# Eleven result sums from accumulating transfers to VectorE, and shorter engine costs in a list scheduler, in a fused attention and MLP kernel

## The chip, the cores and the metric

The kernel runs on one core of a Trainium2 chip. The metric is the device time of one execution in microseconds. Three executions of the kernel before took 1354.43, 1355.80 and 1355.89 us; the median is 1355.8 us.

## The reference

Inputs are q, k, v (8 batches, 8 heads, 576 tokens, 64 wide), phi (32 memory slots) and four weight matrices. All is float32.

```
a = softmax(phi over the 32 slots); k_m = a^T k; v_m = a^T v        # per batch and head
x = softmax(q k_m^T / 8) v_m                                        # 4608 tokens x 512
h = x @ w_in;  g = s * relu(h)^2 + b;  x = g @ w_out                # 512 -> 2048 -> 512
h = x @ moe2_w_in;  g = h * sigmoid(1.702 h);  out = g @ moe2_w_out # 512 -> 2048 -> 512
```

## The kernel before, in words

The work has four stages. Stage 1 does the attention and the first product (batch by batch), stage 2 the second matrix, stage 3 the third, stage 4 the fourth, which gives `out`. In stages 2 to 4 the tokens go in N = 6 blocks `s` of 768 (two halves of TS = 384), and the matrix product of a block is made from products of half-size blocks, with sums and differences of the operands ahead and of the results behind, so that fewer products are needed. Each product is made of three matmuls per tile (high part by high, high by low, low by high), since the operands are split into a rounded part `oh` and a rest `ol` (`operand`, with `hi` on ScalarE or VectorE and `lo` on VectorE, L275, L276 and L281).

In stage 4 the method `last` (one call per block) places the products 1, 6, 7, 5, 3 and 4 of the block. The middle blocks (1 to 4) take the order 1, 6, 7, 5, Y, A, 4, B, D of the table MID, where Y, A, B and D are the steps of a product that a pair of neighbouring blocks shares (`phase4`). Products 1, 6, 5 and 3 add up in the PSUM tile X, products 7 and 4 in the PSUM tile Y, the shared steps in the PSUM tile Z. A pass of the table is 58.5 / 7 = 8.36 us long in the plan.

What leaves PSUM is written in `leaves` (one call per product) and at the end of `phase4`. In the kernel before:

- after product 1, 6, 5 or 3, ScalarE copies X to the tiles a, u2, u4 or c12 (L1235), and SyncE's queue sends them to `out` (L265);
- after product 7 ScalarE copies Y to the tile y7 (L1242; two halves at L1245 in the last block), which is sent to the quarter (1, 1) of `out`. After product 5 the tile u4 is added onto that same quarter by an accumulating transfer (`onto`, L270), issued from POOL's queue;
- after product 6 the tile u2 is sent to the quarter (1, 0), and after product 4, in all blocks but the last, ScalarE copies Y to the tile y4 and a second accumulating transfer adds it there. In the last block VectorE adds Y to u2 in two halves, and these are sent;
- the shared product Z is copied to tiles z by ScalarE (L1344, L1347) and added to `out` by 29 accumulating transfers of 192 KB. The change leaves these as they are.

So there are 11 accumulating transfers of whole quarters (384 KB each): 6 of u4 and 5 of y4.

The order of all instructions on all engines and queues is made by the class `Order` when the program is built: a list scheduler. Every operation has a due time, one or more ways (an engine with a cost in us), what it reads and writes, and the SBUF or PSUM tiles that it needs. `Order.sort` walks through time, asks for each ready operation when its engine, its operands and its tiles will be free, and takes the earliest; the due times break ties. `FIRST` (100) lowers the rank of operations that empty PSUM, so that they come ahead of others. Tiles of SBUF come from two pools: 30 of weights ("w") and 33 of all else ("t"). A tile counts as free when the end of its last use is past. The end of an operation is its start, its cost and an extra: 3.0 us for SyncE's transfers ("sync") and 5.0 us for accumulating transfers ("acc"), 0 for the others. For "acc" the cost is KB / 200: 0.96 us for 192 KB. Costs of ScalarE and VectorE come from `act` and `dve`. A wrong estimate does no harm to the result, since every real wait is on semaphores; but each engine's queue keeps the order that the plan gave it.

Of the kernel before, what the change touches and what calls it, by code (L numbers as in the profile page):

```python
# [15 lines left out]
ALU = mybir.AluOpType  # L16
AX = mybir.AxisListType
PSUM = bass.MemoryType.PSUM
P = 128
# [8 lines left out]
class Order:  # L28
# [7 lines left out]
    FILL, AHEAD, SLACK = 2.5, 190.0, 0.3  # L36

    NEAR = 10

    LAG = {"pe": 0.7, "sync": 2.5, "acc": 2.5, "dve": 0.25, "act": 0.25, "pool": 0.25}  # L40
    WEIGHT = {"dve": 2.0, "pool": 1.6, "act": 1.0}

    def __init__(self, bufs):
# [24 lines left out]
    def sort(self):  # L68
# [13 lines left out]
        at, end, on, out = {}, [0.0] * len(ops), [None] * len(ops), []  # L82
# [8 lines left out]
        while ready:  # L91
            can = {}
            limit = ready[0][0] + self.AHEAD
            for due, n in ready:
                if due > limit and can:
                    break
                _, ways, deps, new = ops[n]
                t0 = 0.0
                if new:
                    ok = True  # L100
                    for tag in {x[0] for x in new}:
                        mine = [x for x in new if x[0] == tag]
                        f = free[tag]
                        if len(f) < len(mine) or any(x not in queue[tag][:len(f)] for x in mine):
                            ok = False
                            break
                        t0 = max(t0, f[0] if len(mine) == 1 else heapq.nsmallest(len(mine), f)[-1])
                    if not ok:
                        continue
                best = None  # L110
                for i, (eng, cost, _, port) in enumerate(ways):
                    t = max(t0, at.get(eng, 0.0))
                    if port:
                        t = max(t, held["dve" if eng == "pool" else "pool"])
                    for d in deps:
                        e = end[d] + (self.LAG[eng] if on[d] != eng else 0.05)
                        if e > t:
                            t = e
                    score = t + cost * self.WEIGHT.get(eng, 1.0)
                    if best is None or score < best[0]:  # L120
                        best = score, t, eng, i
                can.setdefault(best[2], []).append((best[1], due, n, best[3]))
            if not can:
                raise RuntimeError("no order")
            first = []
            for tag, v in can.items():
                t0 = min(v)[0]
                like = [c for c in v if c[0] <= t0 + 0.1 and c[2] in self.narrow and c[1] >= self.since] if tag == "pe" and run else ()
                if like:
                    c = min(like, key=lambda c: c[1:])  # L130
                    if c[1] < min(v, key=lambda c: c[1:])[1] + self.NEAR:
                        first.append(c)
                        continue
                first.append(min((c for c in v if c[0] <= t0 + (self.SLACK if c[1] < self.until else 0.0)), key=lambda c: c[1:]))
            t, _, n, i = min(first)
            _, ways, _, new = ops[n]
            eng, cost, fn, port = ways[i]
            if port:
                held[eng] = t + cost
            if self.fill and eng == "pe":  # L140
                out.append(lambda n=int((t - at.get(eng, 0.0)) * self.FILL): self.fill and self.fill(n))
            for x in new:
                queue[x[0]].remove(x)
                heapq.heappop(free[x[0]])
            at[eng], on[n] = t + cost, eng
            end[n] = t + cost + (3.0 if eng == "sync" else 5.0 if eng == "acc" else 0.0)
            ready.remove((rank[n], n))
            if eng == "pe":
                run = n in self.narrow
            out.append(fn)  # L150
            for m in after[n]:
                left[m] -= 1
                if not left[m]:
                    bisect.insort(ready, (rank[m], m))
            for x in of[n]:
                last[x] = max(last[x], end[n])
                uses[x] -= 1
                if not uses[x]:
                    heapq.heappush(free[x[0]], last[x] + 0.2)
# [5 lines left out]
class Net:  # L165
# [33 lines left out]
    TS, N = 384, 6  # L199
# [48 lines left out]


    def act(self, n, fn, psum=False, count=1):  # L250
        return "act", count * ((166 if psum else 195) + 0.835 * n) / 1e3, fn, False

    def dve(self, n, fn, fast=False, count=1, port=False):
        return "dve", count * (120 + 0.6 * n if fast else (150 + 1.045 * n) if port else (60 + 1.04 * n)) / 1e3, fn, port

    def pe(self, due, n, fn, r=(), w=(), count=0, narrow=False):

# [52 lines left out]
    def convert(self, due, key, out, src, lead=6, pool=True):  # L310
# [10 lines left out]
        def size(act):  # L321
            H = T[raw][:, :, 1]
            m = to["m"] = out().bitcast(U32)
            if act:
                nc.scalar.activation(m.bitcast(F32), H.bitcast(F32), AF.Abs)
            else:
                nc.vector.tensor_scalar(m, H, 0x7FFFFFFF, None, op0=ALU.bitwise_and)

        def low(act):
            L = T[raw][:, :, 0]  # L330
            if act:
                nc.scalar.activation(L, L, AF.Copy, scale=2.0 ** -29)
            else:
                nc.vector.tensor_scalar(L, L, 2.0 ** -29, None, op0=ALU.mult)
# [827 lines left out]
    HEAD = {1: -2, 6: 0, 7: 1, 5: 2, "Y2": 3, 3: 4.5, 4: 5.5}  # L1162
    MID = {1: -3, 6: 0, 7: 1.25, 5: 2.25, "Y": 3.25, "A": 4.75, 4: 5.25, "B": 6.25, "D": 7.75}
    END = {1: -3, 6: 0, 7: 1.25, 5: 2.25, "A2": 3.25, 3: 3.75, "B2": 4.75, 4: 5.25, "D2": 5.75}
    AHEAD, OD, CC, RAW = 10, 6, 5, 4
    LONG = {"Y": 0.5, "A": 0.5, "B": 0.5, "D": 0.25}
    EARLY, LEAD, BEGIN, T4 = 8, 8, -2, -6.3

# [58 lines left out]
    def leaves(self, s, i, X, Ys, d):  # L1227

        nc, T, TS = self.nc, self.T, self.TS
        n = 2 * TS  # L1230
        a, u2, u4, c12 = (("t", (x, "w2", s)) for x in ("a", "u2", "u4", "c12"))
        alone = s in (0, self.N - 1)

        def copy(k):
            self.on_act(d, n, lambda: nc.scalar.copy(self.two(k), T[X][:, :, 0:TS]), (X,), ((*k, 0), (*k, 1)), self.FIRST, psum=True)  # L1235

        def send(k, i, j):
            self.dma(d + 1, lambda: self.a["out"][s, i, j], lambda: T[k].rearrange("p a b -> p (a b)"), ((*k, 0), (*k, 1)), (("out", s, i, j),), 384)

        def seven(k):  # L1240
            if Ys[0] == Ys[1]:
                self.on_act(d, n, lambda: nc.scalar.copy(self.two(k), T[Ys[0]][:, :, 0:TS]), (Ys[0],), ((*k, 0), (*k, 1)), self.FIRST, psum=True)  # L1242
                return
            for o in range(2):
                self.on_act(d, TS, lambda o=o: nc.scalar.copy(self.get(k, [P, 2, TS])[:, o], T[Ys[o]][:, o, 0:TS]), (Ys[o], *(((*k, 0),) if o else ())), ((*k, o),), self.FIRST, psum=True)  # L1245

        def plus(k, i, j):
            self.onto(d + 1, lambda: self.a["out"][s, i, j], lambda: T[k].rearrange("p a b -> p (a b)"), ((*k, 0), (*k, 1)), (("out", s, i, j),))

        y7, y4 = (("t", ("y", "w2", s, i)) for i in (7, 4))  # L1250
        if i == 1:
            copy(a)
            if s < self.N - 1:
                send(a, 0, 0)
            else:
                self.dma(d + 1, lambda: self.a["out"][s, 0, 0][:, TS:2 * TS], lambda: T[a][:, 1], ((*a, 1),), (("out", s, 0, 0),), 192)
        elif i == 6:
            copy(u2)
            if Ys[0] == Ys[1]:
                send(u2, 1, 0)  # L1260
        elif i == 7:
            seven(y7)
            send(y7, 1, 1)
        elif i == 5:
            copy(u4)
            if not alone:
                send(u4, 0, 1)
            plus(u4, 1, 1)
        elif i == 3:
            copy(c12)  # L1270
            send(c12, 0, 1)
        elif i == 4 and Ys[0] == Ys[1]:
            seven(y4)
            plus(y4, 1, 0)
        elif i == 4:
            for o in range(2):
                self.tt(d, TS, lambda o=o: T[u2][:, o], lambda o=o: T[Ys[o]][:, o, 0:TS], lambda o=o: T[u2][:, o], ALU.add, (Ys[o],), ((*u2, o),), self.FIRST)
                self.dma(d + 1, lambda o=o: self.a["out"][s, 1, 0][:, o * TS:o * TS + TS], lambda o=o: T[u2][:, o], ((*u2, o),), (("out", s, 1, 0, o),), 192)

    def phase4(self, s, m, w, due, st, G):  # L1280
# [258 lines left out]
```

## Time and profile before

| | before |
|---|---|
| median of three runs | 1355.8 us |
| time of the profiled execution | 1355.95 us |
| its span (first to last instruction) | 1354.2 us |
| PE (matmuls) busy | 1333.3 us, 98% |
| VectorE (DVE) busy | 1112.5 us, 82% |
| ScalarE (ACT) busy | 865.2 us, 64% |
| GpSimd (POOL) busy | 87.3 us, 6% |
| mean transfer rate | 284 GB/s |

Busy times are sums over instructions that overlap with those of other engines, so they don't add up to the span. The busy time of PE counts a matmul from its start to its modelled end; a busy PE is one that had a matmul in work. The transfer that an instruction of POOL's queue issues is carried out later by the DMA engines: from issue to landing. In the trace, the stages begin at about 0, 297, 644 and 997 us.

### The profile page before, as it was taken

The numbers are of one execution on the slowest core, as the hardware profiler recorded it, in microseconds if no ns is written. First come the engines' busy times: TensorE is split into PE (matmuls) and PEld (weight loads), VectorE is DVE, ScalarE is ACT, GpSimd is POOL, SyncE is SP. The second block draws the span as 40 slices with busy tenths as digits, with TensorE's granted clock in tenths as the row PEclk, the third lists the DMA queues.
The fourth block names the chain that finished last, engine by engine and source line by source line (L and its number), as shares of the span: only waits on it lengthen the run. The fifth ranks groups of instructions, "written<-read, shape, count | busy, mean of one in ns | idle before, by whom it ended". The sixth has DMA issues, their size and how long they took to land. (4 is left out here: it accounts for less than half of the span.)

```text
span 1354.2 us, 24210 instructions
## 1 busy us (share of the span) xinstructions
PE 1333.3 (98%) x9078; PEld 1290.1 (95%) x9078; DVE 1112.5 (82%) x1615; ACT 865.2 (64%) x1213; POOL 87.3 (6%) x82
## 2 busy tenths in 40 slices
PE   7999999999999999999999999999999999999998
PEld 5888888899999999999999999999999999999998
DVE  6878996999898897989986898695477688888885
ACT  4766666788887888778654665575455455646544
POOL 2201220200000000000000000000000011101011
PEclk8999999999999999999999999999999999999999
DMA  9989999797865785498999799889999788778974
GB/s 362 354 307 345 360 342 323 267 320 267 283 192 172 227 295 164 168 354 320 382 342 353 255 345 336 321 308 334 344 332 345 227 240 248 205 221 228 285 203 92
DMA packets 151349, 384.81 MB, mean 284 GB/s; under 512 B 16832, under 2 KB 27712, under 8 KB 151232
## 3 DMA queue, kind: packets, MB, share of 16 engines
q1 hardware_dynamic: 145472, 373.24, 78.2%
q0 software_dynamic: 5760, 10.03, 5.0%
q8 instruction: 71, 1.16, 0.4%
q14 instruction: 46, 0.38, 0.1%
HBM read 232.41 MB, written 150.80 MB: 283 GB/s over the span
## 5 line engine op out<-in xcount | busy, mean ns | idle before, releaser
L305 PE MATMUL h<-ah,mh 128*128 128x288 f32 x512 | 154.6, 302 | 0.2 <-DVE ml L281 0.2
L307 PE MATMUL h<-ah,ml 128*128 128x288 f32 x512 | 151.1, 295 | 0.2 <-ACT ml L815 0.2
L306 PE MATMUL h<-al,mh 128*128 128x288 f32 x512 | 150.7, 294 | 0.0
L281 DVE TENSOR_TENSOR ol<-A,oh 128x768 fp32r<-128x768 f32 x120 | 112.5, 953 | 28.9 <-ACT oh L275 14.4
L932 PE MATMUL X<-oh,wo 128*128 128x384 f32 x384 | 128.3, 334 | 0.0
L933 PE MATMUL X<-ol,wo 128*128 128x384 f32 x384 | 128.3, 334 | 0.0
L934 PE MATMUL X<-oh,wo 128*128 128x384 f32 x384 | 128.3, 334 | 0.0
L1080 PE MATMUL X<-oh,w 128*128 128x384 f32 x384 | 128.3, 334 | 0.0
L1081 PE MATMUL X<-ol,w 128*128 128x384 f32 x384 | 128.3, 334 | 0.0
L1082 PE MATMUL X<-oh,w 128*128 128x384 f32 x384 | 128.3, 334 | 0.0
L275 ACT CAST oh<-A 128x768 fp32r<-128x768 f32 x116 | 98.1, 860 | 44.1 <-DVE A L281 8.4
L834 ACT ACTIVATE r<-h 128x576 f32<-128x576 f32 x122 | 85.8, 706 | 56.0 <-PE h L307 47.7
L1216 PE MATMUL X<-oh,w 128*128 128x384 f32 x320 | 107.0, 334 | 0.8 <-ACT u L1235 0.8
L305 PEld LDWEIGHTS h<-ah,mh 128*128 128x128 f32 x512 | 96.1, 188 | 11.5 <-issue 3.6
L1218 PE MATMUL X<-oh,w 128*128 128x384 f32 x320 | 106.9, 334 | 0.0
L1217 PE MATMUL X<-ol,w 128*128 128x384 f32 x288 | 96.4, 335 | 1.4 <-DVE ol L281 1.4
L307 PEld LDWEIGHTS h<-ah,ml 128*128 128x128 f32 x512 | 96.1, 188 | 0.4 <-ACT ml L815 0.4
L306 PEld LDWEIGHTS h<-al,mh 128*128 128x128 f32 x512 | 96.1, 188 | 0.1
L275 ACT CAST oh<-B 128x768 fp32r<-128x768 f32 x70 | 59.2, 855 | 42.3 <-DVE B L281 19.0
L275 ACT CAST oh<-C 128x768 fp32r<-128x768 f32 x67 | 58.0, 875 | 35.2 <-DVE C L281 12.5
L281 DVE TENSOR_TENSOR ol<-B,oh 128x768 fp32r<-128x768 f32 x72 | 67.7, 953 | 9.1 <-DMA out<-z 5.6
L1380 ACT ACTIVATE u<-u 128x768 f32<-128x768 f32 x48 | 40.7, 848 | 50.4 <-DVE u L281 50.4
(294 smaller groups left out, 3871.9 us busy)
## 6 DMA issues: line engine op xcount, KB each, us to landing
w<-w SPq DMA_DIRECT2D x132, 512.0 KB, 5.7
r<-r SPq DMA_DIRECT2D x128, 288.0 KB, 4.1
kv<-in_kv SPq DMA_DIRECT2D x72, 258.0 KB, 5.2
g<-u SPq DMA_DIRECT2D x48, 384.0 KB, 4.1
raw<-in_w SPq DMA_DIRECT2D x32, 512.0 KB, 5.9
q<-in_q SPq DMA_DIRECT2D x32, 288.0 KB, 5.6
A<-r SPq DMA_DIRECT2D x24, 384.0 KB, 4.6
B<-r SPq DMA_DIRECT2D x24, 384.0 KB, 4.8
```

The lines of the kernel that those rows point to most:

```text
L275: self.order.add(due, [self.act(n, lambda: nc.scalar.copy(out(), src()), psum), self.dve(n, lambda: nc.vector.tensor_copy(out(), src()), f ...
L281: self.order.add(due, [self.dve(n, lambda: nc.vector.tensor_tensor(out(), a(), b(), op=op), port=port)], r, w, first)
L305: self.nc.tensor.matmul(ps, wh, xh, start=start and i == 0, stop=False)
L306: self.nc.tensor.matmul(ps, wh, xl, start=False, stop=False)
L307: self.nc.tensor.matmul(ps, wl, xh, start=False, stop=(i == n - 1))
L932: nc.tensor.matmul(out, T[w][:, 0, c], T[h][:, p], start=f, stop=False, skip_group_check=True)
L933: nc.tensor.matmul(out, T[w][:, 0, c], T[l][:, p], start=False, stop=False, skip_group_check=True)
L934: nc.tensor.matmul(out, T[w][:, 1, c], T[h][:, p], start=False, stop=last, skip_group_check=True)
L1080: nc.tensor.matmul(out, T[w][:, 0, c], T[h][:, k], start=f, stop=False, skip_group_check=True)
L1081: nc.tensor.matmul(out, T[w][:, 0, c], T[l][:, k], start=False, stop=False, skip_group_check=True)
L1082: nc.tensor.matmul(out, T[w][:, 1, c], T[h][:, k], start=False, stop=k == 1, skip_group_check=True)
L1216: nc.tensor.matmul(out, T[w][:, 0, c], T[h][:, p], start=f, stop=False, skip_group_check=True)
```

## The change

The plan's costs for ScalarE and VectorE are shortened, and ends get a table of their own:

```diff
+    END_LAG = {"sync": 3.0, "acc": 8.0, "dve": 0.09, "act": 0.09}
...
-            end[n] = t + cost + (3.0 if eng == "sync" else 5.0 if eng == "acc" else 0.0)
+            end[n] = t + cost + self.END_LAG.get(eng, 0.0)
...
-        return "act", count * ((166 if psum else 195) + 0.835 * n) / 1e3, fn, False
+        return "act", count * ((100 if psum else 110) + 0.835 * n) / 1e3, fn, False
...
-        return "dve", count * (120 + 0.6 * n if fast else (150 + 1.045 * n) if port else (60 + 1.04 * n)) / 1e3, fn, port
+        return "dve", count * (50 + 0.6 * n if fast else (75 + 1.045 * n) if port else (60 + 1.04 * n)) / 1e3, fn, port
...
-    AHEAD, OD, CC, RAW = 10, 6, 5, 4
+    AHEAD, OD, CC, RAW = 11, 6, 5, 3
```

AHEAD and RAW are lead times in the due times of loads: a pair's older block is due 1 us earlier, the loads of the operands C and D 1 us later.

In `leaves`, the copies of Y and the accumulating transfers of u4 and y4 go; VectorE adds Y to the tile instead, and one plain transfer takes the sum out:

```diff
-        alone = s in (0, self.N - 1)
+        alone, b5 = s in (0, self.N - 1), ("t", ("b5", "w2", s))
...
-        def seven(k):
+        def plus(k, to):
             if Ys[0] == Ys[1]:
-                self.on_act(d, n, lambda: nc.scalar.copy(self.two(k), T[Ys[0]][:, :, 0:TS]), (Ys[0],), ((*k, 0), (*k, 1)), self.FIRST, psum=True)
+                if to == k:
+                    self.tt(d, n, lambda: T[k], lambda: T[Ys[0]][:, :, 0:TS], lambda: T[k], ALU.add, (Ys[0],), ((*k, 0), (*k, 1)), self.FIRST)
+                else:
+                    self.tt(d, n, lambda: self.two(to), lambda: T[Ys[0]][:, :, 0:TS], lambda: T[k], ALU.add, (Ys[0], (*k, 0), (*k, 1)), ((*to, 0), (*to, 1)), self.FIRST)
                 return
             for o in range(2):
...
+                self.tt(d, TS, lambda o=o: T[k][:, o], lambda o=o: T[Ys[o]][:, o, 0:TS], lambda o=o: T[k][:, o], ALU.add, (Ys[o],), ((*k, o),), self.FIRST)
...
-        def plus(k, i, j):
-            self.onto(d + 1, lambda: self.a["out"][s, i, j], lambda: T[k].rearrange("p a b -> p (a b)"), ((*k, 0), (*k, 1)), (("out", s, i, j),))
...
         elif i == 6:
             copy(u2)
-            if Ys[0] == Ys[1]:
-                send(u2, 1, 0)
-        elif i == 7:
-            seven(y7)
-            send(y7, 1, 1)
         elif i == 5:
             copy(u4)
-            if not alone:
+            if alone:
+                plus(u4, u4)
+                send(u4, 1, 1)
+            else:
                 send(u4, 0, 1)
-            plus(u4, 1, 1)
+                plus(u4, b5)
+                send(b5, 1, 1)
...
-        elif i == 4 and Ys[0] == Ys[1]:
-            seven(y4)
-            plus(y4, 1, 0)
         elif i == 4:
+            plus(u2, u2)
+            if Ys[0] == Ys[1]:
+                send(u2, 1, 0)
+                return
             for o in range(2):
```

So after product 7 nothing leaves PSUM; after product 5 the sum Y + u4 is made (in u4 itself in the first and last block, in a new tile b5 in the others, where u4 is sent on its own too); after product 4 the sum Y + u2 is made in u2, which is no longer sent after product 6.

## Rows read from the trace of the kernel before

**Rows 1.** Windows by stage, then one stretch of stage 4: window, length, busy time (instructions) by engine

```profile
core 0: us, PE busy (x) PEld busy (x) DVE busy (x) ACT busy (x) POOL busy (x), PEclk, DMA share, GB/s
0.00:50.00 50.00, 39.14 (x334) 32.43 (x334) 37.78 (x64) 29.66 (x49) 12.47 (x14) 0.86 0.92 344
50.00:308.00 258.00, 257.08 (x2760) 223.75 (x2759) 219.69 (x346) 176.89 (x265) 39.61 (x28) 1.00 0.94 329
308.00:997.00 689.00, 688.91 (x3994) 688.50 (x3994) 569.85 (x831) 471.51 (x644) 0.00 (x0) 1.00 0.82 289
997.00:1354.20 357.20, 348.12 (x1997) 345.43 (x1995) 285.24 (x376) 187.15 (x256) 35.26 (x40) 1.00 0.79 234
1205.00:1230.00 25.00, 23.39 (x134) 22.75 (x133) 25.00 (x39) 15.69 (x24) 2.60 (x4) 1.00 0.68 190
```

**Rows 2.** Waits of PE in stage 4: total us, times, longest

```profile
PE Z L1330 <- DVE ol L281: 1.6, 2, 0.9
PE X L1217 <- DVE ol L281: 1.4, 1, 1.4
PE Z L1329 <- ACT z L1347: 1.1, 2, 0.9
PE X L1216 <- ACT u L1235: 0.8, 1, 0.8
PE Z L1329 <- ACT u L1235: 0.3, 1, 0.3
```

**Rows 3.** Chain that ended last, pieces of stage 4: start us, us, what

```profile
1196.03 7.80 issue
...
1212.49 1.74 DVE ol L281 x2
...
1218.43 0.45 PE Z L1330
...
1236.87 4.23 issue
...
1262.12 6.48 DMA out<-y
...
1286.86 9.76 DMA out<-z
...
1350.49 0.56 DVE a L281
```

**Rows 4.** Timeline of POOL in stage 4: start, us, issue [idle before <-releaser]

```profile
1195.69 0.89 POOL L270 DMA_DIRECT2D out<-z  x1 [10.66 <-ACT z L1347]
...
1234.33 0.88 POOL L270 DMA_DIRECT2D out<-y  x1 [3.42 <-ACT y L1242]
```

**Rows 5.** Timeline of ACT, 1082 to 1100 us

```profile
1090.65 0.80 ACT L1242 COPY y<-Y 128x768 f32<-128x768 f32 x1 [7.92 <-DMA out<-u]
...
1095.52 0.80 ACT L1235 COPY u<-X 128x768 f32<-128x768 f32 x1 [1.36 <-DMA out<-y]
```

**Rows 6.** Groups of VectorE and ScalarE in stage 4, by form: busy us, mean ns | idle before

```profile
L281 DVE TENSOR_TENSOR u<-Y,u 128x768 f32<-128x768 f32 x2 | 1.9, 954 | 0.9 <-PE Y L1082 0.9
...
L275 ACT CAST oh<-A 128x768 fp32r<-128x768 f32 x66 | 54.2, 836 | 41.0 <-DVE A L281 8.4 <-issue 7.8 <-PE Y L1217 4.8
...
L1242 ACT COPY y<-Y 128x768 f32<-128x768 f32 x10 | 8.0, 798 | 10.2 <-DMA out<-u 7.9 <-PE Y L1218 2.2
L1245 ACT COPY y<-Y 128x384 f32<-128x384 f32 x2 | 1.0, 476 | 0.0
```

**Rows 7.** Transfers by issue: queue, count, KB each, median us to landing

```profile
out<-z POOLq DMA_DIRECT2D x29, 192.0 KB, 5.3
...
out<-y POOLq DMA_DIRECT2D x5, 384.0 KB, 6.7
```

**Rows 8.** Waits of VectorE in stage 4 for a load: total us, times, longest

```profile
DVE A L281 <- DMA C<-g: 9.1, 6, 3.1
```

**Rows 9.** Waits of VectorE in stage 3 (640 to 997 us)

```profile
DVE ab L281 <- PE Z L1151: 29.7, 16, 4.2
...
DVE u L281 <- PE Y L1082: 4.1, 15, 0.8
```

More of the change, by code (lines that the diff above doesn't have):

```diff
@@ L1238, in send @@
             self.dma(d + 1, lambda: self.a["out"][s, i, j], lambda: T[k].rearrange("p a b -> p (a b)"), ((*k, 0), (*k, 1)), (("out", s, i, j),), 384)
-        def seven(k):
+        def plus(k, to):
             if Ys[0] == Ys[1]:
-                self.on_act(d, n, lambda: nc.scalar.copy(self.two(k), T[Ys[0]][:, :, 0:TS]), (Ys[0],), ((*k, 0), (*k, 1)), self.FIRST, psum=True)
+                if to == k:
+                    self.tt(d, n, lambda: T[k], lambda: T[Ys[0]][:, :, 0:TS], lambda: T[k], ALU.add, (Ys[0],), ((*k, 0), (*k, 1)), self.FIRST)
+                else:
+                    self.tt(d, n, lambda: self.two(to), lambda: T[Ys[0]][:, :, 0:TS], lambda: T[k], ALU.add, (Ys[0], (*k, 0), (*k, 1)), ((*to, 0), (*to, 1)), self.FIRST)
                 return
             for o in range(2):
-                self.on_act(d, TS, lambda o=o: nc.scalar.copy(self.get(k, [P, 2, TS])[:, o], T[Ys[o]][:, o, 0:TS]), (Ys[o], *(((*k, 0),) if o else ())), ((*k, o),), self.FIRST, psum=True)
-        def plus(k, i, j):
-            self.onto(d + 1, lambda: self.a["out"][s, i, j], lambda: T[k].rearrange("p a b -> p (a b)"), ((*k, 0), (*k, 1)), (("out", s, i, j),))
-        y7, y4 = (("t", ("y", "w2", s, i)) for i in (7, 4))
+                self.tt(d, TS, lambda o=o: T[k][:, o], lambda o=o: T[Ys[o]][:, o, 0:TS], lambda o=o: T[k][:, o], ALU.add, (Ys[o],), ((*k, o),), self.FIRST)
         if i == 1:
@@ L1271, in leaves @@
             send(c12, 0, 1)
-        elif i == 4 and Ys[0] == Ys[1]:
-            seven(y4)
-            plus(y4, 1, 0)
         elif i == 4:
+            plus(u2, u2)
+            if Ys[0] == Ys[1]:
+                send(u2, 1, 0)
+                return
             for o in range(2):
-                self.tt(d, TS, lambda o=o: T[u2][:, o], lambda o=o: T[Ys[o]][:, o, 0:TS], lambda o=o: T[u2][:, o], ALU.add, (Ys[o],), ((*u2, o),), self.FIRST)
                 self.dma(d + 1, lambda o=o: self.a["out"][s, 1, 0][:, o * TS:o * TS + TS], lambda o=o: T[u2][:, o], ((*u2, o),), (("out", s, 1, 0, o),), 192)
```

## The prediction, made before the result was known

> **What bounds the kernel now.** I read the windows by stage first, since 98% busy for the whole says nothing of where the rest lies. Between 308 and 997 us PE is busy 688.91 of 689.00 us [rows 1]: 3994 matmuls, one every 0.172 us, nothing to gain. Stage 1 after its start loses 0.92 us of 258. The first 50 us lose 10.86 us while the first loads and the first batch's attention come in. Stage 4 loses 9.08 us of 357.20, and the chain ends in VectorE's last sum at 1351.05 and its transfer [rows 3], so that some 4 us of these lie behind the last matmul. PE's waits in stage 4 are the rest: 1.6 + 1.4 + 1.1 + 0.8 + 0.3 = 5.2 us in 7 waits [rows 2]. The chain also shows that the first matmul after a wait takes 0.45 us in place of 0.17 [rows 3], 0.28 us more, so the 7 waits cost 5.2 + 7 x 0.28 = 7.2 us. That is the most that stage 4 can give.
>
> Next, what stands behind each wait. The chain shows ScalarE held for 4 to 10 us at a time by transfers that still read the tile which ScalarE is to write [rows 3]; VectorE then starves and afterwards works off a backlog, and PE meets the backlog.
> - **Group A, transfers of y and u4's path**: ScalarE's copy of y waits 7.92 us for a transfer of u, and the copy of u behind it 1.36 us for one of y [rows 5]; PE loses 0.8 there [rows 2]. ScalarE's 4.23 us up to 1241.10 [rows 3] end 6.8 us after POOL issued the accumulation of y at 1234.33 [rows 4], whose median landing is 6.7 us [rows 7]; PE loses 0.2 of the 1.1 in rows 2. A plain transfer of y, 6.48 us [rows 3], is behind the 0.3. Sum 1.3 us and 3 x 0.28: 2.1 us.
> - **Group B, accumulations of z**: ScalarE's 7.80 us of "issue" up to 1203.83 [rows 3] name no releaser; they end 8.1 us after z was issued at 1195.69 [rows 4], and I put them down to it. VectorE is then busy for 25.00 of 25 us [rows 1], and PE waits twice, 1.6 us. The 9.76 us of z from 1286.86 [rows 3] stand behind 0.9 + 1.4 us. Sum 3.9 us and 4 x 0.28: 5.1 us (rounding aside, the two groups make 7.2).
>
> **The change part by part.** The profiled execution took 1355.95 us, 0.15 above the median, with a span of 1354.2; I sum against 1355.95 and take 0.15 off.
>
> *Copies and accumulations removed.* Ten copies of 798 ns and two halves of 476 ns [rows 6] leave ScalarE: 8.9 us of an engine that is idle for 357.20 - 187.15 = 170 us in stage 4 [rows 1]. That alone is worth nothing on PE's path. Eleven accumulations leave POOL's queue, 5 of y [rows 7] and 6 of u4, with 4.3 MB each of reads and writes of `out`; no tile of y or y4 exists any more that ScalarE could wait for. Group A goes: -2.1 us. Between nothing (another transfer takes the tile's place) and -2.1 I take -2.1, as three waits of three name it.
>
> *Sums added.* Ten sums of 768 columns and two halves go to VectorE, reading PSUM. The nearest row is the same sum at the end of stage 3: 954 ns [rows 6]; issued back to back VectorE takes 1.74 / 2 = 0.87 us per operation of this width [rows 3]. 11 x 0.87 = 9.6 us, of 357.20 - 285.24 = 72 us in which VectorE was idle [rows 1]. Each stands at the head of VectorE's queue until PE ends its product, and what is queued behind (the rests `ol` and the differences for the next products, for which ScalarE and PE wait) stands too. In stage 3 such sums waited 4.1 / 15 = 0.3 us for Y, and those on Z 29.7 / 16 = 1.9 us [rows 9]. So they take between 11 x 1.2 = 13 and 11 x 2.8 = 31 us of the 72. While VectorE has slack that costs PE nothing; within a catch-up like 1205 to 1230 us each 0.87 goes through. Ends: 0 and +7 (eight sums in four middle blocks, all through). I take +0.9, one sum of the eleven, since catch-ups follow from the very stalls that go.
>
> *Tiles.* u2 is now kept from product 6 to product 4, some five passes of 8.36 us of the plan, where y7 and y4 lived for some 10 us each: about half a tile of 33 more in use on average. Loads wait for tiles, and VectorE waits for loads (9.1 us in 6 waits for C [rows 8]). A half tile in 33 is 1.5%; the cover is VectorE's idle time. 0, with ends 0 and +1. The lead times AHEAD and RAW move loads by 1 us in opposite directions and count with this.
>
> *Queues.* SyncE's queue sends as many quarters as before; POOL's queue no longer holds z behind u4 and y4. Nothing on PE's path.
>
> *The reckoning.* Old costs equal durations: 195 + 0.835 x 768 = 836 ns for a cast, as in rows 6. New ones equal distances: 75 + 1.045 x 768 = 878 ns, against the 0.87 us of rows 3. So the plan drifts less from the chip. For accumulations of z it now holds the tile for 0.96 + 8 = 9.0 us from issue, not 6.0. The three holds above lasted 6.8, 8.1 and 9.8: two of them would have ended inside the 9.0, none inside the 6.0. That speaks to group B. Ends: 0 and -5.1; I take 0.6 of it, -3.1, as the 9.76 of the pair that cost most still exceeds 9.0, and which free tile is given out is not by the plan's own estimate.
>
> The Trainium skill, on the page "DMA: Bandwidth & Descriptors", section "Anatomy of one DMA — SWDGE (gpsimd) path", gives about 2.0 us and bytes / 436 GB/s for a transfer issued from GpSimd, which an estimate makes 2.5 us for 192 KB. By it the old 5 us were ample, the 8 would buy nothing, and the sum would lose its -3.1. The trace differs: a median of 5.3 us for z [rows 7] and 9.76 at the longest [rows 3].
>
> *Stages 1 to 3.* All orders are made anew, though no operation of these stages changes. Stage 2 and 3 have nothing to lose but their cover (VectorE 83% busy). The start, with 10.86 us idle, can move either way. I take 0, with ends -2 and +4 (three waits of 1.4, the longest of rows 2).
>
> *The tail.* The last block's product 4 was summed on VectorE before already: 0.
>
> Sum: -2.1 + 0.9 - 3.1 = -4.3: 1355.95 - 4.3 - 0.15 = 1351.5 us.
>
> **The rivals.**
> 1. *Only y's stalls go.* The accumulations of z hold ScalarE as before; 29 of 40 remain and the page's rule above would have it that the longer reserve is worth nothing. For it: the longest hold exceeds even 9.0 us. Against: two of three don't. -2.1: 1353.7 us.
> 2. *All stalls go.* For it: with 4.3 MB less in the slow queue z lands sooner. -7.2: 1348.6 us.
> 3. *New waits elsewhere.* A new order in 24,000 instructions opens as many waits as it closes, at the start or in stage 1. For it: the old costs, too long, left margin. Against: stages 2 and 3 have 17% of VectorE to spare. Three waits of 1.4 us on top of the forecast: 1355.7 us.
> 4. *VectorE becomes the bound (slower).* The sums stand at the head of VectorE's queue in the middle blocks, where a backlog is being worked off; from the point where the backlog is longer than the lead of the next product's operands, every 0.87 us goes to PE. 8 x 0.87 = 7.0, less 2.1: +4.9, 1360.7 us. For it: 25 us of VectorE without a gap, and the 1.9 us waits of stage 3. Against: 80% busy over the stage, and 83% is carried without loss in stage 3, which sums on VectorE in the same way.
>
> That the edit does something else can be left aside: both accumulations are gone from the code for every block.
>
> **How the numbers follow.** A measurement here can tell about 0.2%, 2.7 us: faster is below 1353.1, slower above 1358.5. Forecast (-2.7 to -6) 0.42, rival 2 0.13: faster 0.55. Rival 1 0.22, rival 3 0.11: same 0.33. Rival 4 0.12. The range goes from all stalls gone and a start better by 1 us, 1347.5, to rival 3 with 2 us more, 1357.5; it leaves out rival 4 and little else.
>
> **What would show it.** In the changed trace: no transfers out<-y, 29 accumulations left; PE's waits in stage 4 near 2 us in place of 5.2, none of them behind y; sums u<-Y and b<-Y on VectorE at 0.87 to 0.95 us. Z's landing above 9 us with ScalarE held by it speaks for rival 1. VectorE above 85% busy in stage 4, with PE waiting for `ol` behind a sum, speaks for rival 4. A first 50 us with PE busy well below 39 us, or gaps in stages 2 and 3, speak for rival 3. PE's waits in stage 4 no shorter than before would make the prediction wrong.

## The result: 1.4% slower, and the profile after

The changed kernel takes 1373.89 us (median; 1371.77 to 1378.75), the kernel before beside it 1355.12 us (1354.37 to 1355.89): a ratio of 1.0144 with a 95% interval of 1.0113 to 1.0174. The forecast was 1351.5, its range ended at 1357.5, and its sign was wrong. The profiled execution of the changed kernel took 1375.49 us.

The page of the changed kernel, its span, the busy time of each engine, and the queue of POOL's transfers (packets, MB, share):

```profile
span 1373.7 us, 24220 instructions
PE 1342.7 (98%) x9088; PEld 1296.6 (94%) x9088; DVE 1130.5 (82%) x1634; ACT 851.4 (62%) x1194; POOL 78.1 (6%) x71
...
q0 software_dynamic: 4176, 5.70, 3.1%
```

The edit did what it says: POOL's queue moves 5.70 MB, some 4.3 MB less than before, and 29 accumulations are left, all of z. The shares do not show where 19.5 us more of span come from. The windows by stage do (columns as in [rows 1]):

```profile
0.00:50.00 50.00, 41.46 (x365) 33.80 (x366) 39.24 (x64) 31.51 (x54) 12.43 (x14) 0.90 0.95 351
50.00:308.00 258.00, 257.04 (x2745) 223.94 (x2744) 224.92 (x353) 176.25 (x264) 39.92 (x28) 1.00 0.94 328
308.00:997.00 689.00, 687.82 (x3983) 686.85 (x3982) 570.49 (x831) 465.15 (x636) 0.00 (x0) 1.00 0.82 288
997.00:1373.70 376.70, 356.34 (x2001) 352.04 (x1999) 295.87 (x389) 178.48 (x243) 25.71 (x29) 0.98 0.68 212
```

Up to 997 us the two kernels are level: PE is busy 2.3 us more in the first 50 and 1.1 us less in the stretch from 308 to 997. Stage 4 takes 376.70 us against 357.20 [rows 1]; 19.5 us, all of the loss. It has 20.4 us without PE in place of 9.1, and a mean clock of 0.98. VectorE is 295.87 / 376.70 = 79% busy, as before.

PE's waits in stage 4, changed kernel (total us, times, longest), which answer to [rows 2]:

```profile
PE X L1218 <- DVE ol L282: 5.4, 5, 2.4
PE X L1217 <- ACT u L1236: 4.9, 2, 4.0
PE X L1217 <- ACT oh L276: 2.9, 2, 2.0
PE X L1218 <- DVE D L282: 2.2, 1, 2.2
PE Z L1328 <- ACT z L1346: 0.9, 1, 0.9
PE X L1217 <- ACT z L1346: 0.3, 1, 0.3
```

16.6 us in 12 waits, against 5.2 in 7. With 0.28 us for each restart these are 20.0 us against 7.2, which explains 12.8 of the 19.5. Most of the rest is clock. The matmuls around the two waits that end at 1272 and 1278 us (start, duration, idle before):

```profile
1272.32 0.44 PE L1218 MATMUL X<-ol,w 128*128 128x384 f32 x1 [2.38 <-DVE ol L282]
...
1276.09 0.33 PE L1218 MATMUL X<-ol,w 128*128 128x384 f32 x1
1276.27 0.34 PE L1219 MATMUL X<-oh,w 128*128 128x384 f32 x1
1278.60 0.69 PE L1217 MATMUL X<-oh,w 128*128 128x384 f32 x1 [2.00 <-ACT oh L276]
1279.59 0.69 PE L1218 MATMUL X<-ol,w 128*128 128x384 f32 x1 [0.31 <-DVE ol L282]
1280.08 0.52 PE L1219 MATMUL X<-oh,w 128*128 128x384 f32 x1
1280.40 0.52 PE L1217 MATMUL X<-oh,w 128*128 128x384 f32 x1
...
1285.48 0.34 PE L1218 MATMUL X<-ol,w 128*128 128x384 f32 x1
1285.66 0.33 PE L1219 MATMUL X<-oh,w 128*128 128x384 f32 x1
```

Before 1276.27 a matmul starts every 0.17 us; after the waits, every 0.32. Read the starts, since the durations overlap. Windows of the same kernel around the three places where this happens show the clock:

```profile
1145.00:1150.00 5.00, 2.78 (x12) 2.20 (x12) 3.40 (x5) 0.59 (x2) 0.86 (x1) 0.89 0.85 246
1150.00:1155.00 5.00, 4.14 (x17) 3.69 (x15) 0.33 (x1) 1.20 (x2) 0.00 (x0) 0.77 0.63 187
...
1220.00:1225.00 5.00, 4.92 (x19) 4.92 (x20) 5.00 (x9) 1.96 (x5) 0.86 (x1) 0.66 0.50 163
...
1280.00:1285.00 5.00, 5.00 (x17) 5.00 (x17) 4.72 (x10) 0.94 (x2) 0.00 (x0) 0.50 0.10 20
```

From 1280 to 1285 the granted clock is 0.50, the lower of the two levels, 1.2 GHz: PE is "busy" for 5.00 of 5.00 us and does 17 matmuls in place of 29. Some 40 matmuls of stage 4 ran like this, each 0.15 us late: 5.9 us. In 1000 to 1345 us of before's stage 4 no 5 us were granted less than full speed. So a few long waits cost more than their length, and the busy share hides that part.

**What makes PE wait** stands two engines further back. ScalarE's waits in stage 4, changed kernel:

```profile
ACT oh L276 <- issue: 24.6, 3, 8.3
ACT oh L276 <- DVE ol L282: 24.0, 6, 8.3
```

Three times ScalarE stands for 8 us before a cast, and the trace names no releaser. Its timeline around the first, then that of VectorE and of POOL:

```profile
1139.28 0.83 ACT L276 CAST oh<-B 128x768 fp32r<-128x768 f32 x1 [8.31 <-DVE ol L282]
...
1145.12 0.47 ACT L1346 COPY z<-Z 128x384 f32<-128x384 f32 x1
1153.80 1.56 ACT L276 CAST oh<-A 128x768 fp32r<-128x768 f32 x2 [8.21 <-issue]
```

```profile
1138.29 0.96 DVE L282 TENSOR_TENSOR ol<-B,oh 128x768 fp32r<-128x768 f32 x1 [4.49 <-DMA out<-z]
...
1154.67 0.96 DVE L282 TENSOR_TENSOR ol<-A,oh 128x768 fp32r<-128x768 f32 x1 [6.26 <-ACT oh L276]
```

```profile
1145.94 0.86 POOL L271 DMA_DIRECT2D out<-z  x1 [13.59 <-ACT z L1346]
...
1204.56 0.88 POOL L271 DMA_DIRECT2D out<-z  x1 [10.87 <-ACT z L1346]
...
1269.77 0.89 POOL L271 DMA_DIRECT2D out<-z  x1 [12.84 <-ACT z L1346]
```

Read them together. ScalarE copies a half product into z at 1145.12; POOL issues its accumulation at 1145.94; by the trace's semaphore updates that lands at 1153.74; at 1153.80 ScalarE goes on. The other two landed at 1212.89 and 1277.65, and ScalarE went on at 1212.95 and 1277.71: 0.06 us after the landing each time. The addresses in the built program say why: the cast `oh` behind the copy of z was given the very tile that the accumulation of z still reads. Where VectorE's `ol` gets such a tile, VectorE itself stands, as at 1138.29. Whenever that happened in the changed kernel, three to six other tiles were out of use in the order in which the program is written. The plan of the order does not see it: it reckons with a tile that is free by then and plans 1.0 us of idle PE in stage 4, for both kernels.

So the kernel before has the same holds ([rows 3, 5] show some of them). By the addresses, 17 of the 19 tiles of z were handed on early in either kernel, that is at a time at which, by the plan itself, the accumulation had not ended: to 11 operations of ScalarE and VectorE in the kernel before, to 12 in the changed one, and the rest to loads. In the kernel before, 10 more operations of the two engines were given a tile that an accumulation of u4 or y4 still read; in the changed kernel none. So the count of such hand-outs did not rise. What is left as the difference is where in the work they fall, and the runs below test that.

### The profile page after: what moved, and what is told of

Same layout as the page of the kernel before. It is cut to its first block, busy times and chain, and to the rows that moved or that the text cites. A ratio compares the mean times of both kernels' runs of the same rounds, so it can differ in the third digit from the quotient of the medians.

```text
span 1373.7 us, 24220 instructions
## 1 busy us (share of the span) xinstructions
PE 1342.7 (98%) x9088; PEld 1296.6 (94%) x9088; DVE 1130.5 (82%) x1634; ACT 851.4 (62%) x1194; POOL 78.1 (6%) x71
## 3 DMA queue, kind: packets, MB, share of 16 engines
HBM read 232.41 MB, written 146.47 MB: 276 GB/s over the span
## 4 chain that ended last, share of the span: by engine, by line
PE 83%; issue 6%; DVE 4%; DMA 4%; ACT 3%; POOL 0%; SPq 0%; ACTq 0%; DVEq 0%; POOLq 0%
PE X L935 5%; PE X L933 5%; PE X L934 5%; PE h L306 5%; PE X L1081 5%; PE X L1083 5%; PE X L1082 5%; PE h L308 4%; PE h L307 4%; PE X L1218 3%; PE X L1219 3%; PE X L1217 3%; PE Y L935 2%; PE Y L933 2%; PE Y L934 2%
## 5 line engine op out<-in xcount | busy, mean ns | idle before, releaser
L276 ACT CAST oh<-A 128x768 fp32r<-128x768 f32 x111 | 94.5, 866 | 72.7 <-issue 24.6
L1081 PE MATMUL X<-oh,w 128*128 128x384 f32 x384 | 128.6, 335 | 1.2 <-ACT u L1093 0.7
L1082 PE MATMUL X<-ol,w 128*128 128x384 f32 x384 | 128.3, 334 | 0.0
L1083 PE MATMUL X<-oh,w 128*128 128x384 f32 x384 | 128.3, 334 | 0.0
L1217 PE MATMUL X<-oh,w 128*128 128x384 f32 x320 | 110.1, 344 | 8.1 <-ACT u L1236 4.9
L1219 PE MATMUL X<-oh,w 128*128 128x384 f32 x320 | 109.5, 342 | 0.0
L1218 PE MATMUL X<-ol,w 128*128 128x384 f32 x288 | 99.2, 344 | 5.4 <-DVE ol L282 5.4
L271 POOL DMA_DIRECT2D out<-z x29 | 25.7, 992 | 1079.7 <-DVE z L282 913.1
```

The lines of the kernel that those rows point to most:

```text
L276: self.order.add(due, [self.act(n, lambda: nc.scalar.copy(out(), src()), psum), self.dve(n, lambda: nc.vector.tensor_copy(out(), src()), f ...
L1081: nc.tensor.matmul(out, T[w][:, 0, c], T[h][:, k], start=f, stop=False, skip_group_check=True)
L1082: nc.tensor.matmul(out, T[w][:, 0, c], T[l][:, k], start=False, stop=False, skip_group_check=True)
L1083: nc.tensor.matmul(out, T[w][:, 1, c], T[h][:, k], start=False, stop=k == 1, skip_group_check=True)
L1217: nc.tensor.matmul(out, T[w][:, 0, c], T[h][:, p], start=f, stop=False, skip_group_check=True)
```

## The experiments

Three theories. **T** (tiles): the holds by transfers of z decide, and any new order draws their places anew. **S** (sums): the sums on VectorE are the price (rival 4 of the prediction). **R** (reckoning): the new reckoning is, by its shorter costs. In all, the kernel before, run beside each group, took 1353.7 to 1353.9 us.

**1. The changed kernel with z in tiles of its own.** Two tiles that hold nothing but z, 31 for the rest.

```
-    BUFS = {"w": 30, "t": 33, ...
+    BUFS = {"w": 30, "t": 31, "z": 2, ...
-        k, c = ("t", (f"z{w}", s, m)), len(plan)
+        k, c = ("z", (f"z{w}", s, m)), len(plan)
```

> The changed kernel, with the tiles of z (the shared products' results, which 29 accumulating transfers read) in a pool of their own of 2, and 31 tiles in place of 33 for all else. Theory T (tiles): in the changed kernel ScalarE and VectorE are held some 8 us at a time because the tile that they are to write is one that an accumulation of z still reads; PE's 16.6 us of waits in stage 4 and the fall of its clock come from that. Then those holds go, and PE's waits in stage 4 fall to 2 to 6 us: 1352 to 1359 us. Theory S (sums): the sums at the head of VectorE's queue cost the time; they are unchanged, so 1368 to 1378 us. Theory R (reckoning): the shorter costs make an order without margin, unchanged here: 1368 to 1378 us.

Measured: 1354.24 us, ratio 1.0000 (0.9987 to 1.0013). All sums and the new reckoning are in it, and the loss is gone. PE's waits in its stage 4:

```profile
PE X L1218 <- DVE ol L282: 1.0, 2, 0.8
PE Z L1329 <- DVE ol L282: 0.2, 1, 0.2
```

1.2 us in place of 16.6. Its price is in stages 2 and 3, where 31 tiles are scarce: PE is busy 685.92 us from 308 to 997, in place of 688.91 [rows 1].

**2. The kernel before with z in tiles of its own** (the same edit).

> The kernel before, with the tiles of z in a pool of their own of 2 (31 for all else); its 11 accumulations of u4 and y4 stay in the common pool. Theory T: group B of the prediction (5.1 us behind accumulations of z) goes, less what two tiles fewer cost: 1350 to 1356 us. Theories S and R: 1354 to 1357 us, no change, as neither the sums nor the costs are in it.

Measured: 1354.87 us, 1.0012 (1.0001 to 1.0023). 3.8 us of waits in stage 4, and 3.3 us lost in stages 2 and 3: here the tiles cost what they bring. The time lies in the ranges of all three theories, so this run does not tell them apart.

**3. The changed kernel with the old reckoning.** The sums and the leads stay, the costs and ends are those of before.

```
-    END_LAG = {"sync": 3.0, "acc": 8.0, "dve": 0.09, "act": 0.09}
+    END_LAG = {"sync": 3.0, "acc": 5.0}
-        ... ((100 if psum else 110) + 0.835 * n) ...
+        ... ((166 if psum else 195) + 0.835 * n) ...
-        ... (50 + 0.6 * n if fast else (75 + 1.045 * n) if port ...
+        ... (120 + 0.6 * n if fast else (150 + 1.045 * n) if port ...
```

> The changed kernel with the old costs of ScalarE and VectorE and the old ends (accumulations 5 us, the two engines 0): the sums on VectorE alone, with the new lead times. Theory S: the sums still cost the time, 1366 to 1378 us. Theory R: the loss goes with the new reckoning, 1351 to 1357 us. Theory T: the loss depends on which operations are handed a tile of z, so anything from 1353 to 1372 us, with ScalarE's long waits ending where a transfer of z lands.

Measured: 1371.94 us, 1.0123 (1.0097 to 1.015). R falls: without the new reckoning it is as slow. The waits have moved, though. The largest of its 13.9 us in stage 4, then ScalarE's timeline before one of them:

```profile
PE Z L1328 <- ACT z L1346: 7.9, 3, 3.7
PE Z L1329 <- DVE ol L282: 2.7, 1, 2.7
```

```profile
1125.63 0.83 ACT L276 CAST oh<-B 128x768 fp32r<-128x768 f32 x1 [5.93 <-DMA out<-z]
1126.37 0.79 ACT L1346 COPY z<-Z 128x768 f32<-128x768 f32 x1
```

The cast was held for 5.93 us by a transfer of z, the copy of Z behind it came late, and PE, which needs Z emptied, went on at 1127.22 after 3.75 us.

**4. The kernel before with the new reckoning,** its sums where they were (the inverse of the edit of 3, on the kernel before).

> The kernel before with the new costs and ends alone: no sum moved, 40 accumulations. Theory R: slower by 10 us and more, 1365 to 1380 us. Theory S: 1352 to 1357 us. Theory T: as many tiles handed on while an accumulation reads them as before, so 1353 to 1370 us.

Measured: 1367.62 us, 1.0106 (1.0082 to 1.0131), with 8.8 us of waits in stage 4. No sum has been moved and yet it is 1% slower: S falls as the only cause. ScalarE's casts were held by transfers of z here too:

```profile
ACT oh L275 <- DMA out<-z: 18.4, 5, 8.2
```

Either half of the change makes most of the loss, and the two together no more than one: not two costs that add up, but a draw that is made again.

**5. The changed kernel with 31 tiles,** z among them: the control for 1.

```
-    BUFS = {"w": 30, "t": 33, ...
+    BUFS = {"w": 30, "t": 31, ...
```

> The changed kernel with 31 tiles in place of 33 in the common pool and nothing else: the control for the run with z apart, which had 31 too. If that run won by its new order or by the smaller pool (theory R), this one wins too: 1351 to 1358 us. Theory T: the tiles of z are still handed on while an accumulation reads them, so it stays slow, 1362 to 1385 us.

Measured: 1371.25 us, 1.0126 (1.0106 to 1.0146). PE's waits in stage 4 are 12.9 us, where run 1 has 1.2. So in 1 it was the tiles of its own, not the smaller number of the others.

**6. The kernel before with 32 tiles** (one less, nothing else).

> The kernel before with 32 tiles in place of 33: a new order with nothing else changed. Theory T, with the addition that the kernel before had an order in which the holds happened to fall where PE had work in store: the luck goes, 1360 to 1378 us. If the kernel before is robust and the change alone does the harm (theory S): 1354 to 1359 us.

Measured: 1373.01 us, 1.0139 (1.0119 to 1.0159), as slow as the changed kernel without a line of the change. Its largest group of PE's waits, and one hold of ScalarE, in whose row the trace names the transfer:

```profile
PE X L1216 <- ACT u L1235: 8.1, 3, 4.3
```

```profile
1318.40 0.83 ACT L275 CAST oh<-B 128x768 fp32r<-128x768 f32 x1 [8.16 <-DMA out<-z]
```

Some 3.6 us of PE's time are lost between 308 and 997 us, where the tile is missing (685.27 us busy, in place of 688.91); most of the rest is in stage 4. This is the strongest run for T's second half: an edit that does little but shift the order can give the whole loss.

**7. The changed kernel with z in a ring:** the copies of z take turns in two fixed tiles of the 33, by name.

```
-        k, c = ("t", (f"z{w}", s, m)), len(plan)
+        k, c = ("t", ("zr", self.turn % 2)), len(plan)
+        self.turn += 1
...
-  ... nc.scalar.copy(self.two(k)[:, 0:c], ...
+  ... nc.scalar.copy(self.get(k, [P, 2, TS])[:, 0:c], ...
```

> The changed kernel with 33 tiles, where all copies of z share two fixed tiles of the common pool, turn about, from the first copy of z on; so no other operation is handed a tile of z, and stages 1 to 3 keep 33. Theory T: 1350 to 1355 us, PE's waits in stage 4 below 5 us. Theories S and R: 1365 to 1378 us.

Measured: 1352.66 us, 0.9993 (0.9984 to 1.0003); some 20 us less than the changed kernel. PE's waits in stage 4 are 1.9 us:

```profile
PE X L1218 <- DVE ol L282: 1.3, 2, 0.7
PE Y L1218 <- DVE ol L282: 0.6, 1, 0.6
```

**8. The kernel before with the ring and the new reckoning.**

> The kernel before with the new reckoning and z in two fixed tiles; its 11 accumulations of u4 and y4 stay in the common pool and can still hold ScalarE. Theory T: most of the 13 us that the new reckoning alone cost goes, 1352 to 1361 us. Theory R: still 1363 to 1373 us.

Measured: 1355.76 us, 1.001 (0.9998 to 1.0022). With the ring the new reckoning costs nothing that can be told; without it, in 4, it cost 14 us.

**9. The changed kernel, z written plainly.** Order and addresses are those of the changed kernel; only the length of the holds differs.

```
-  ... nc.gpsimd.dma_start(out(), in_(), accum_op=ALU.add)
+  ... nc.gpsimd.dma_start(out(), in_())
```

> The changed kernel with the same instructions in the same order on every engine and the same tile addresses; only the 29 transfers of z from POOL's queue write their 192 KB plainly and don't add (the adding of the shared products to the output is left out). Theory T: the plain transfers land sooner, in 2.5 to 5 us in place of 3.5 to 8.7, ScalarE's three holds of 8.1 to 8.3 us shorten to 3 to 5, and PE's 16.6 us of waits in stage 4 fall to 3 to 10: 1355 to 1366 us. Theories S and R: the order and the sums are the same, so 1369 to 1379 us.

Measured: 1351.7 us, 0.999 (0.9979 to 1.0001): lower than I expected. ScalarE's timeline at the place that was shown above, and PE's waits in stage 4:

```profile
1139.82 0.47 ACT L1346 COPY z<-Z 128x384 f32<-128x384 f32 x1
1144.30 0.84 ACT L276 CAST oh<-A 128x768 fp32r<-128x768 f32 x1 [4.01 <-issue]
```

```profile
PE X L1218 <- DVE D L282: 0.4, 1, 0.4
```

The same copy, the same cast behind it, the same tile: a hold of 4.01 us in place of 8.21, and PE waits 0.4 us in all in place of 16.6. The loss doesn't grow with the hold in proportion: what the engines had in store at these places covered some 4 us, and not 8. This run also lightens the DMA engines (share in stage 4: 0.66, against 0.73 in 7 with the adding) and can't hold that apart from the shorter holds; 1 and 7 keep the adding and lose nothing either.

**10. The sums and the ring, with the old reckoning** (the edits of 3 and 7).

> The sums on VectorE with the old reckoning, and z in two fixed tiles. Theory T: with no tile of z handed on, the 18 us that the same sums cost with shared tiles go: 1352 to 1361 us. Theory S: the sums cost the time with any tiles, 1366 to 1376 us.

Measured: 1354.53 us, 1.0011 (1.0 to 1.0022), 2.6 us of waits in stage 4.

**11. The kernel before with the ring,** nothing of the change.

> The kernel before with z in two fixed tiles, old costs, no sum moved. Theory T: a new order that no longer needs luck, save for its 11 accumulations of u4 and y4 which stay in the common pool: 1351 to 1358 us. If any new order of the kernel before is slow (as the one with 32 tiles was, 1373 us): 1364 to 1376 us.

Measured: 1352.31 us, 0.999 (0.9979 to 1.0002), 2.6 us of waits in stage 4. With the ring, then, the four combinations give 1352.31 (neither part), 1354.53 (sums), 1355.76 (reckoning) and 1352.66 (both). 10 and 11 ran beside each other: the sums came out at 2.2 us, 0.2%, at the bound of what can be told, and with the new reckoning (7 and 8, beside each other) at -3.1. That is no price of the sums. (The lead times AHEAD and RAW go with the sums in all runs, and the reserve of 8 us goes with the shorter costs; none of them was run alone.)

**12. The ring with other leads,** the edit of 7 and:

```
SLACK 0.3 -> 0.2   NEAR 10 -> 15   WEIGHT dve 2.0 -> 2.4
T4 -6.3 -> -6.6    AHEAD 11 -> 12   OD 6 -> 7   CC 5 -> 7
```

> The changed kernel with z in two fixed tiles and other settings of the scheduler (SLACK 0.2, NEAR 15, WEIGHT of VectorE 2.4, T4 -6.6, AHEAD 12, OD 7, CC 7): one more new order. Theory T: with no tile of z handed on, a new order is no lottery any more, so within 3 us of the ring run's 1352.7 us: 1349.5 to 1355.5, and perhaps the first that is clear of the kernel before. If orders still scatter as they did with shared tiles: anything from 1353 to 1375 us.

Measured: 1351.83 us, 0.9984 (0.9975 to 0.9993), the only ratio whose interval lies below 1. PE's waits in its stage 4:

```profile
PE X L1217 <- ACT u L1236: 1.0, 1, 1.0
PE X L1218 <- DVE ol L282: 0.2, 1, 0.2
```

It is faster than the kernel before by about 2 us, 0.16%, which is inside the 0.2% that the prediction called no change, and than the changed kernel by some 20. Seven constants differ at once; which of them counts, and whether it is better than 7 (whose interval overlaps), isn't settled.

**Taken together.** Six orders with z among the common tiles: 1353.8 (the kernel before), 1367.6, 1371.3, 1371.9, 1373.0 and 1373.9. Seven with z apart or in a ring: 1351.8 to 1355.8. The mean granted clock of stage 4 was 0.98 or 0.99 in the five slow orders and 1.00 in all others. T stands. Three things stay open. By which rule the tile is chosen when several are free wasn't tried. In 2, 8 and 11, eight to eleven operations of ScalarE and VectorE were still given a tile of u4 or y4 under accumulation, and nothing was lost that can be told; why these holds are covered isn't shown. And whether the kernel before came by its good order by luck or by the tuning of its constants is not on record.

## Why the prediction was wrong

- **What bounds the kernel.** PE's waits behind holds of ScalarE by transfers: right, and the 7.80 us that I "put down" to z did end with its landing, at 1203.77 against ScalarE's start at 1203.83. But I took each hold for what it cost in this order. In the kernel before 21 operations of ScalarE and VectorE are given a tile that an accumulation still reads, and PE pays for few; the rows of PE's waits only showed those that did not happen to be covered.
- **Copies and accumulations removed, -2.1.** The removal took place: no transfer of y, no hold by one, and 146.47 MB written in place of 150.80 (the page's count of reads, 232.41 MB, is the same for both kernels, so reads of `out` don't show there). Its gain can't be seen, since the loss by new holds is some nine times as large. Nor did z land sooner, as rival 2 had it: its median is 5.3 us in both kernels.
- **Sums added, +0.9.** The sums themselves were sized well; what their new order did was not. The sums on VectorE after 997 us in the changed kernel, by form, and the halves in the kernel before:

```profile
L282 DVE TENSOR_TENSOR u<-Y,u 128x768 f32<-128x768 f32 x8 | 7.6, 954 | 0.4 <-PE Y L1219 0.4
...
L282 DVE TENSOR_TENSOR b<-Y,u 128x768 f32<-128x768 f32 x4 | 3.8, 954 | 0.0
L282 DVE TENSOR_TENSOR u<-Y,u 128x384 f32<-128x384 f32 x4 | 2.1, 554 | 11.1 <-PE Y L1219 11.1
```

```profile
L281 DVE TENSOR_TENSOR u<-Y,u 128x384 f32<-128x384 f32 x2 | 1.1, 558 | 11.1 <-PE Y L1218 11.1
```

  954 ns, as forecast, and the twelve wide ones (two of them the last of stage 3) wait 0.4 us in all. The four halves wait 11.1 us, but the two of the kernel before waited as long. With z in a ring the sums cost nothing that can be told (runs 7 and 10: 1352.66 and 1354.53). With shared tiles and the old reckoning, run 3, they and their leads come with +18 us, far beyond the +7 at the end of this term: the term had no price for a new order. Rival 4 had the right sign and the wrong place: VectorE at 79%, under the 85 that I had set for it.
- **The reckoning, -3.1: the step that failed.** It argued that holding z's tile for 9.0 us, not 6.0, covers landings of 6.8 and 8.1 us. One reading in it was wrong: the 6.8 was y's, 384 KB, for which the old plan held 384 / 200 + 5 = 6.9 us already, so of z's two holds only one would have ended inside the 9.0. The landings of z behind the changed kernel's three holds are of the size read: 7.79, 8.33 and 7.87 us after the issue, all inside the 9.0. But the reserve governs only the plan's own account of free tiles, and not which address is handed out: with either reserve 17 of 19 tiles of z were handed on early. The text said so, "which free tile is given out is not by the plan's own estimate", and used it to take 0.6 of the gain. It should have been the mechanism, with a loss at its end: the ends of that term were 0 and -5.1, and run 4, this part alone, measured +14, while with z in a ring (run 8) the same part left the time at 1355.76, where the loss is gone. What the prediction had wrong is thus the wait that it priced: not the holds of z that PE met in the old order, but those that any new order uncovers.
- **Tiles, 0 to +1.** Wrong likewise: one tile of 33 less, and nothing else, cost 19 us in run 6. Want of room is the smaller part of it (some 3.6 us there, and 3.0 in run 1 for two tiles less); the rest comes since it makes a new order.
- **Rival 3, new waits elsewhere,** was the right story at a fifth of its size or less. (Its price with 2 us more is 1357.7, not the 1357.5 of the range, which changes nothing.) Its "three waits of 1.4 us" took the longest wait of before for the longest there can be. Holds of 8 us were in the rows; behind one whose cover is gone PE waited up to 4.0 us, and then ran at the lower clock level, for which no term stood: 5.9 us.
- **Stages 1 to 3** were right: stage 4 starts at 997.78 us in place of 997.11, within the -2 and +4.
- **The longer reserve.** No run changes it alone, but by the addresses it kept no tile of z from being handed on early. The fit in the Trainium skill's "DMA: Bandwidth & Descriptors", section "Anatomy of one DMA — SWDGE (gpsimd) path", from which I had estimated 2.5 us for 192 KB and so no use for the reserve, is not borne out by these landings of 3.5 to 8.7 us. If the reserve bought nothing, as run 4 suggests, it was for the reason above and not for short landings.

## What to carry to other kernels

Where one program plans an order and another hands out the buffers, the plan's idle time is no forecast: give every tile that a slow transfer reads an address of its own, by name, before tuning anything else. In a kernel whose in-order engines stand for 8 us at a time, count the holds that cost nothing today, and price any edit that makes a new order by what they cost uncovered; a control that does little but shift the order (a tile more or less) can tell in one run whether the edit or the new order was measured. And read waits of PE together with the granted clock behind them, since a busy share counts slow matmuls as work.

## What the runs showed of the hardware

- Accumulations into `out` of 192 KB of z, in the changed kernel's stage 4, landed 3.5 to 8.7 us after issue. The same transfers without adding, in run 9, landed after 2.2 to 6.3, and held POOL for 0.54 us each (median) in place of 0.88.
- After waits of 2.38 and 2.00 us, 6.3 us apart, PE's granted clock was 0.51 over the next 6.5 us, with PE busy for 6.10 of them. After one wait of 3.96 us at 1220.08 the matmuls were 0.32 us apart for 3.2 us. I had reckoned a wait of PE at its length and 0.28 us.
